# RWKV-6 attention with a gated MLP: a third unit's output projection by seven half-width products

## The chip, the cores and the metric

One Trainium2 chip, one core of it. The metric is device time in microseconds (us) of one execution of the whole program; lower is better. TensorE (PE) multiplies matrices, with PEld as its weight load; VectorE (DVE), ScalarE (ACT) and GpSimd (POOL) work on tiles; SyncE (SP) issues most of the transfers.

## The reference, cut to what matters

```python
# attention: batch 4, 8 heads, 768 tokens, head size 48
for t in range(S):
    kt, vt, rt, wt = (k[:, :, t], v[:, :, t], r[:, :, t], w[:, :, t])
    cur = np.einsum('bhd,bhe->bhde', u[None] * kt, vt)
    y[:, :, t] = np.einsum('bhd,bhde->bhe', rt, state + cur)
    state = wt[:, :, :, None] * state + np.einsum('bhd,bhe->bhde', kt, vt)
# bridge: x is y as 3072 tokens x 384
h = x @ w_in                                   # 384 -> 2048
sp = np.maximum(h, 0.0) + np.log1p(np.exp(-np.abs(h)))   # softplus
g = h * erf(sp)                                # the gate
return (g @ w_out).astype(np.float32)          # 2048 -> 384
```

All data is float32.

## The kernel before

**Units and steps.** The work is cut into 12 units of 256 tokens (128 tokens of two batches), taken in 12 steps, numbered from 0. Step s computes the attention of unit s. Beside it, the hidden layer of unit s - 1 is multiplied by w_in, its gate is computed, and the output projection (w_out) of unit s - 3 is done. So the third unit, number 2, is projected in step 5. Steps 0 to 4 go through the function attend, later ones through attend_late.

**The order is written out by hand.** Each engine takes its instructions in the order in which the program issues them. The attention of a step calls in_order (step 4) or run_late (later steps) at fixed places, and these work through short strings. In them "P" issues one piece of the projection, "H" one piece of the hidden layer (two of its 16 rows of blocks: 12 records of TensorE, then a copy on ScalarE, L1036), "s" and "e" a softplus and an erf of one chunk on ScalarE (L983, L987, each with a table load), "m" the multiplication of the gate on VectorE (L992), "F" the next part of the preparation of the following step, "S" the blends, "k" a copy of a quarter of the hidden layer into PSUM (L1100). "A" in step 4 advances a gate that is done in larger parts: softplus (L1009), erf (L1012), then the multiplication in two halves (L1016).

**Two ways to project.** Ordinarily (project) the 256 tokens x 2048 hidden values are multiplied by w_out in 32 matrix products, 384 columns wide, for each of the two batches into one PSUM tile; each tile is copied out on ScalarE (L1068) and sent. From unit FAST = 3 on, project_fast does it with seven products of half blocks instead of eight (Strassen's scheme in Winograd's form): 7 x 8 = 56 matrix products, 192 columns wide. For this

- the hidden values need four sums and differences of their quarters, the blends s1, s2, s3, s4 (L1119 to L1125, VectorE, 128x1024 each),
- the weights need three mixed tiles (L1083, on VectorE in step 3) and one difference in place, b12 - b11 in w_out_sb, which ends the use of the plain w_out_sb. It is sent by mixing.send to GpSimd in step 5, at the "G" of the last string,
- the results are partly added up outside PSUM. The two PSUM tiles m0 and m1 are read by copies on ScalarE (L1148, L1153, L1156) and by two additions on VectorE:

```python
        product(m0[:, lo], s3, t3, False)                                  # sixth product
        halves = o[1][:].rearrange("p (k n) -> p k n", k=2)
        nc.vector.tensor_add(halves, halves, m0[:, None, lo].to_broadcast([P, 2, ND]))   # L1162
        nc.sync.dma_start(out=out[i * NJ + 1, c], in_=o[1][:])
        yield
        if s < n_steps - 1:
            product(m1[:, lo], a12, b21, True)                             # seventh product
            nc.vector.tensor_add(o[0][:], o[0][:], m1[:])                  # L1167
```

The pool ps_m has two buffers ("m"). The projection holds both; after it, the first "H" piece of the step takes the buffer of m0 and the second that of m1, and so on in turn.

**Around the projection in a late step**, TensorE's order is: the level products (L557), the larger part of the projection, the last level's products (L557) and spread_blocks (L677), the rest of the projection, the state products (L664, which need kT from VectorE's L723), then eight "H" pieces (L1027, 96 records), and the attention's products with the values (L589). VectorE scales the inputs of the next step (L333), sums up its near terms (L458; GpSimd makes the terms with L468 and L472), and takes in by_tokens, a small table that goes through DRAM once the sums are complete (L506, L508, then L519). GpSimd also makes the totals (L407) and fades the state (L947, L964).

The functions that the change touches, as they are before:

Of the kernel before, what the change touches and what calls it, by code (L numbers as in the profile page):

```python
# [15 lines left out]
ALU = mybir.AluOpType  # L16

P = 128
FAST = 3
EP = 64  # L20
HC = 64
NC = 2
# [39 lines left out]
def kernel(  # L62
# [14 lines left out]
    nc = tc.nc  # L77
# [916 lines left out]
    def hidden(of, xT, gs, cut):  # L994


        def activate(h):

            held = []

            def softplus():
                n = 2 * (rooms["next"] % 2)
                rooms["next"] += 1
                held.append(
                    room[:, n : n + 2].rearrange("p i n -> p (i n)").rearrange(
                        "p (f t) -> p f t", t=UNIT
                    )
                )
                nc.scalar.activation(held[0], h[:], AF.Softplus)  # L1009

            def erf():
                nc.scalar.activation(held[0], held[0], AF.Erf)  # L1012

            def multiply():
                for part in (slice(0, FG // 2), slice(FG // 2, FG)):
                    nc.vector.tensor_mul(h[:, part], h[:, part], held[0][:, part])  # L1016

            later.extend([(softplus, True), (erf, True), (multiply, False)])

        for g in range(NG):  # L1020
            h = hid.tile([P, FG, UNIT], FP32, name="h")
            gs.append(h)
            for f in range(0, FG, FT):
                ps = ps_m.tile([P, FT, UNIT], FP32, name="m")
                for ff in range(FT):
                    for kk in range(KT):
                        nc.tensor.matmul(  # L1027
                            ps[:, ff, :],
                            lhsT=w_in_sb[:, g * FG + f + ff, kk * P : (kk + 1) * P],
                            rhs=xT[:, kk, :],  # L1030
                            start=kk == 0,
                            stop=kk == KT - 1,
                        )
                    if cut and not ff and g == NG - 1 and f == FG - FT:
                        yield
                nc.scalar.copy(h[:, f : f + FT, :], ps[:])  # L1036
                if of >= FAST:
                    if f % (2 * FT):
                        chunks.append(h[:, f - FT : f + FT])
                elif f == FG - FT:  # L1040
                    activate(h)
                yield
# [249 lines left out]
    def advance(count=None):  # L1292

        while later and count != 0:
            stage, last = later.pop(0)
            stage()
            count = count and count - 1
            if last and not count:
                break
# [20 lines left out]
    def in_order(s, k):  # L1320


        order = ("APPP", "APPP", "APPHH", "AHHH", "AHHH")
        for what in order[k]:
            if what == "A":
                advance()
            elif what == "P":
                piece(projs, s - 3)
            else:
                piece(hids, s - 1)  # L1330
# [2 lines left out]
    STAGES_LATE = ("front", "near", 0, 1, 2, 3, 4)  # L1333
    LATE = {
        DIRECT + 1: (
            "s ey", "m", "s ep m P P s ey m P P P", "s P F ep m P F P k22y k11p F", "S1",
            "S2 S3 H k12y S4 H F", "s H ep m H H F G s H H H ep",
        ),
        n_steps - 1: (
            "s P", "m w", "ey P m s P P ep P", "m P P", "", "", ""  # L1340
# [7 lines left out]
    def run_late(s, tokens, following=None):  # L1348

        for what in tokens.split():  # L1350
            if what == "A":
                advance()
            elif what == "P":
                piece(projs, s - 3)
            elif what == "H":
                piece(hids, s - 1)
            elif what == "F":
                next(following, None)
            elif what == "Q":
                piece(projs, s - 2)  # L1360
            elif what == "J":
                next(turns["joint"])
            elif what == "w":
                next(joining)
            elif what in "uvz":
                activate_pair(what)
            elif what == "T":
                join_tokens()
                turns["joint"] = hidden_of_two()
            elif what == "G":  # L1370
                mixing.send(nc.gpsimd)
            elif what == "s":
                softplus_chunk()
            elif what[0] == "e":
                erf_chunk(what[1])
            elif what == "m":
                multiply_chunk()
            elif what[0] == "k":
                to_lane(s - 2, what[1:3], what[3])
            else:  # L1380
                blend(s - 2, *(int(n) for n in what[1:]))
                if what == "S3":
                    del lanes["11"], lanes["22"]
                elif what == "S4":
                    del lanes["12"]
# [14 lines left out]
    mixing = mix_weights()  # L1400
# [9 lines left out]
    for kk in range(KT):  # L1410
        n = D // KT
        to, of = (x.rearrange("p (e m) -> p e m", e=NE) for x in (apart[:, kk], ident[:]))
        nc.vector.tensor_copy(out=to[:, :, D:], in_=of[:, :, kk * n : (kk + 1) * n])
    load_first()
    with tc.manual_schedule(
# [74 lines left out]
        s = n_steps  # L1490
# [108 lines left out]
```

## Time and profile before

| | us |
|---|---|
| median of three runs | 582.31 (582.29 to 584.92) |
| the profiled execution | 582.34 |
| its span in the trace | 580.6 |
| PE busy | 573.2 (99% of the span) |
| DVE busy | 443.9 (76%) |
| ACT busy | 354.9 (61%) |
| POOL busy | 277.9 (48%) |
| step 4 on TensorE, from its first level products to those of step 5 | 144.2 to 192.7 |
| step 5, from there to the end of its hidden layer | 192.7 to 237.9 |

The profile is of one execution. A line such as "L1027 PE MATMUL m<-xT,w_in_sb" names the line of the kernel, the engine, the operation and the tiles written and read. A float32 matrix product stands in the trace as two records, so 32 products are 64 records. In the chain that ended last, TensorE has 92%.

### The profile page before, as it was taken

The page shows a single profiled execution, that of the slowest core. Times are in us where ns is not written, and L with a number is a line of the kernel's source. Part 1 is how long each engine was busy: PE and PEld are TensorE (multiplying, and loading weights), DVE is VectorE, ACT ScalarE, POOL GpSimd, SP SyncE. Part 2 cuts the span into 40 slices and gives each one's busy share as a digit, 9 for nine tenths or more (in the row PEclk, how much of TensorE's full clock was granted, in tenths as well). Part 3 has the DMA queues.
Part 4 walks back from the last instruction along what each step waited for, and adds up shares of the span by engine and source line. Part 5 has one row for each costly group of instructions (what it writes and reads, how often), then busy time and mean ns, then how long its engine had stood idle before and what let it go on. Part 6 is the DMA issues. An engine that isn't in the chain of part 4 may idle for free.

```text
span 580.6 us, 16629 instructions
## 1 busy us (share of the span) xinstructions
PE 573.2 (99%) x7240; PEld 491.9 (85%) x7240; DVE 443.9 (76%) x539; ACT 354.9 (61%) x478; POOL 277.9 (48%) x313
## 2 busy tenths in 40 slices
PE   8999999999999999999999999999999999999997
PEld 6678887678578668998998898898898899988997
DVE  7775876999994899799799799699699637256640
ACT  3658777644444698766766766766666761388700
POOL 3557391703898389469369359459449100000000
PEclk9999999999999999999999999999999999999999
DMA  8596662340443414234334334333331301000000
GB/s 271 180 313 244 240 202 85 149 148 11 145 150 83 123 43 169 41 138 155 63 126 155 75 119 164 75 113 134 75 109 56 75 8 37 1 0 2 28 27 28
DMA packets 54081, 63.24 MB, mean 109 GB/s; under 512 B 35160, under 2 KB 40568, under 8 KB 52984
## 3 DMA queue, kind: packets, MB, share of 16 engines
q1 hardware_dynamic: 53624, 61.98, 33.4%
q8 instruction: 57, 0.93, 0.7%
q10 hardware_dynamic: 384, 0.20, 0.1%
q14 instruction: 16, 0.13, 0.1%
HBM read 52.39 MB, written 8.69 MB: 105 GB/s over the span
## 4 chain that ended last, share of the span: by engine, by line
PE 92%; DVE 4%; POOL 1%; DMA 1%; issue 1%; ACT 0%; SPq 0%; DVEq 0%; POOLq 0%; ACTq 0%
PE m L1027 34%; PE m L1142 28%; PE m L1059 9%; PE pp L557 5%; PE pp L1230 4%; PE y L1230 2%; PE y L589 2%; PE y L615 2%; PE pp L664 2%; PE m L864 1%; DMA words<-in_moe_w_in 1%; DVE in L333 1%; PE pp L873 1%; PE pp L940 1%; DVE rk L468 1%
## 5 line engine op out<-in xcount | busy, mean ns | idle before, releaser
L1027 PE MATMUL m<-xT,w_in_sb 128*128 128x256 f32 x960 | 215.2, 382 | 0.0
L1027 PEld LDWEIGHTS m<-xT,w_in_sb 128*128 128x128 f32 x960 | 179.9, 190 | 25.8 <-ACT h L1036 1.0
L333 DVE TENSOR_TENSOR in<-in,tot_sb 128x1024 f32<-128x1024 f32 (+1 forms) x55 | 75.2, 1367 | 14.1 <-PE pp L557 11.8
L468 POOL TENSOR_TENSOR rk<-words 128x528 f32<-128x528 f32 (+3 forms) x28 | 42.5, 1517 | 85.1 <-DVE sums L458 81.1
L1036 ACT COPY h<-m 128x512 f32<-128x512 f32 x80 | 46.3, 581 | 59.0 <-PE m L1027 58.9
L472 POOL TENSOR_TENSOR words<-words,rest 128x528 f32<-128x528 f32 (+10 forms) x77 | 78.1, 1014 | 6.0
L1059 PE MATMUL m<-w_out_sb,h 128*128 128x384 f32 x192 | 64.3, 491 | 0.0
L1059 PEld LDWEIGHTS m<-w_out_sb,h 128*128 128x128 f32 x192 | 35.8, 190 | 23.4
L1142 PE MATMUL m<-mixed,h 128*128 128x192 f32 x256 | 45.6, 332 | 0.0
L1142 PE MATMUL m<-w_out_sb,h 128*128 128x192 f32 x256 | 44.8, 329 | 0.0
L1142 PEld LDWEIGHTS m<-mixed,h 128*128 128x128 f32 x256 | 41.4, 190 | 0.9
L1142 PEld LDWEIGHTS m<-w_out_sb,h 128*128 128x128 f32 x256 | 41.6, 190 | 0.3
L1142 PE MATMUL m<-w_out_sb,room 128*128 128x192 f32 x240 | 41.5, 326 | 0.0
L557 PEld LDWEIGHTS pp<-in 48*48 48x48 f32 (+4 forms) x2368 | 30.1, 120 | 12.8 <-issue 5.6
L983 ACT ACT_TABLE_LOAD x30 | 38.5, 1283 | 2.8 <-issue 2.3
L1142 PEld LDWEIGHTS m<-w_out_sb,room 128*128 128x128 f32 x240 | 39.4, 190 | 0.0
L987 ACT ACT_TABLE_LOAD x30 | 38.5, 1283 | 0.5
L468 POOL TENSOR_TENSOR words<-words 128x336 f32<-128x336 f32 (+6 forms) x49 | 35.2, 718 | 3.8
L557 PE MATMUL pp<-in 48*48 48x32 f32 (+4 forms) x2368 | 33.9, 206 | 1.2 <-DVE in L333 1.1
L458 DVE TENSOR_REDUCE sums<-rk 128x14 f32<-128x672 f32 (+9 forms) x54 | 34.7, 701 | 0.0
L407 POOL TENSOR_TENSOR tot_sb<-tot_sb 128x256 f32<-128x256 f32 (+4 forms) x50 | 32.6, 652 | 3.8
L458 DVE TENSOR_REDUCE sums<-words 128x6 f32<-128x288 f32 (+8 forms) x66 | 27.4, 464 | 3.9 <-POOL words L468 3.6
(199 smaller groups left out, 949.8 us busy)
## 6 DMA issues: line engine op xcount, KB each, us to landing
in<-in_rkw SPq DMA_DIRECT2D x8, 1024.0 KB, 5.1
words<-in_moe_w_in SPq DMA_DIRECT2D x16, 384.0 KB, 5.2
words<-in_moe_w_out SPq DMA_DIRECT2D x16, 384.0 KB, 6.3
words<-in_rk_rows SPq DMA_DIRECT2D x8, 768.0 KB, 5.9
w<-in_rkw SPq DMA_DIRECT2D x11, 512.0 KB, 5.5
v<-in_v SPq DMA_DIRECT2D x12, 384.0 KB, 5.4
out<-o SPq DMA_DIRECT2D x23, 192.0 KB, 2.7
in<-in_rkw SPq DMA_DIRECT2D x7, 512.0 KB, 6.3
```

The costliest lines, as they stand in the source:

```text
L333: nc.vector.tensor_mul(halves, halves, view(tots[level - 1], 0, [[1, n], [2, nb], [0, half]]))
L458: nc.vector.tensor_reduce(out=view(sums[:], n, [[near * (NEAR + 1), NEAR // near], [NEAR + 1, near - n]]), in_=terms[n], axis=mybir.AxisLi ...
L468: engine.tensor_mul(terms[n], r[:, :, n:], k[:, :, : near - n])
L472: engine.tensor_mul(k[:, :, :m], k[:, :, :m], w[:, :, n : n + m])
L557: nc.tensor.matmul(to, lhsT=rk(1, n)[rows(e), s0 : s0 + m], rhs=right, start=True, stop=True,)
L983: nc.scalar.activation(sp_room, chunks[0], AF.Softplus)
L987: nc.scalar.activation(at, sp_room, AF.Erf)
L1027: nc.tensor.matmul(ps[:, ff, :], lhsT=w_in_sb[:, g * FG + f + ff, kk * P : (kk + 1) * P], rhs=xT[:, kk, :], start=kk == 0, stop=kk == KT - 1,)
L1036: nc.scalar.copy(h[:, f : f + FT, :], ps[:])
L1059: nc.tensor.matmul(ps[j][:], lhsT=gs[g][:, f, j * C : (j + 1) * C], rhs=w_out_sb[:, g * FG + f, :], start=g + f == 0, stop=g == NG - 1 and ...
L1142: nc.tensor.matmul(to, lhsT=a[:, f], rhs=b[:, f], start=start and f == 0, stop=f == FG - 1, skip_group_check=True,)
L1230: nc.tensor.matmul(to[:, e], lhsT=a[:, 2 * i + e], rhs=b, start=start and not k, stop=True, skip_group_check=True,)
```

## The change

The constant FAST becomes 2, so that unit 2, too, is projected by project_fast, in step 5. A second constant, CHUNKED = 3, keeps the gate of unit 2 as it was (in larger parts). The rest moves what project_fast needs:

- in step 4 the third place runs "APPAAHH" for "APPHH": the second erf is issued there, ahead of the two "H" pieces, and the last two gate multiplications follow at once; the fourth place issues the weight difference ("G", now to VectorE), the fifth the four blends ("B"), where the "A" for erf and multiplications stood;
- in step 5 the strings hold the seven pieces of the short projection for the eight of the ordinary one, and no "G" any more.

```diff
-FAST = 3
+FAST = 2
+CHUNKED = 3
...
-                if of >= FAST:
+                if of >= CHUNKED:
                     if f % (2 * FT):
                         chunks.append(h[:, f - FT : f + FT])
...
-        order = ("APPP", "APPP", "APPHH", "AHHH", "AHHH")
+        order = ("APPP", "APPP", "APPAAHH", "GHHH", "BHHH")
         for what in order[k]:
             if what == "A":
                 advance()
+            elif what == "G":
+                mixing.send(nc.vector)
+            elif what == "B":
+                blend(s - 2)
             elif what == "P":
                 piece(projs, s - 3)
...
         DIRECT + 1: (
-            "s ey", "m", "s ep m P P s ey m P P P", "s P F ep m P F P k22y k11p F", "S1",
-            "S2 S3 H k12y S4 H F", "s H ep m H H F G s H H H ep",
+            "s ey", "m", "P P P s ep m P s ey m P", "s P F ep m F P k22y k11p F", "S1",
+            "S2 S3 H k12y S4 H F", "s H ep m H H F s H H H ep",
         ),
...
-            elif what == "G":
-                mixing.send(nc.gpsimd)
```

Line numbers in the text are those of the kernel before. Instruction by instruction the two programs differ so: TensorE has the 56 half-width products in the place of 32 of full width; VectorE has the weight difference, four blends and two additions more, and two multiplications at another place; ScalarE has three copies (L1148, L1153, L1156) for two (L1068) and the one erf earlier; GpSimd loses the weight difference; SP's two output transfers come from L1163 and L1168.

## The prediction

> **What bounds the kernel now.** I read the page first, then the chain of waits in order of time, then the timelines of VectorE and ScalarE over steps 4 and 5. TensorE is busy for 99% of the span, so the change is worth what it takes from TensorE's row of work, less every hole that it tears into it. The page and then the chain (start, length, what):
>
> ```profile
> PE 573.2 (99%) x7240; PEld 491.9 (85%) x7240; DVE 443.9 (76%) x539; ACT 354.9 (61%) x478; POOL 277.9 (48%) x313
> ```
>
> ```profile
> 193.58 13.10 PE m L1059 x40
> ...
> 207.62 7.94 PE m L1059 x24
> 215.55 0.86 PE pp L664 x64
> 216.42 21.55 PE m L1027 x96
> ...
> 243.56 10.60 PE m L1142 x64
> ...
> 255.09 5.40 PE m L1142 x32
> ...
> 261.35 20.92 PE m L1027 x96
> ```
>
> The first four rows are step 5, the others step 6, which already has the short projection. The hidden layer took 21.55 in step 5, 20.92 in step 6: there are 0.6 us of holes in the former. VectorE's timeline, with the idle time before an instruction and what ended it in brackets:
>
> ```profile
> 170.77 3.85 DVE L1016 TENSOR_TENSOR h<-h,room 128x1024 f32<-128x1024 f32 x2
> ...
> 182.50 0.20 DVE L458 TENSOR_REDUCE sums<-words 128x1 f32<-128x48 f32 x1 [0.57 <-POOL words L468]
> ...
> 188.80 1.23 DVE L519 TENSOR_TENSOR own<-block_sb,by_tokens 128x1024 f32<-128x1024 f32 x1 [1.95 <-DMA by_tokens<-by_blocks]
> 189.94 2.50 DVE L1016 TENSOR_TENSOR h<-h,room 128x1024 f32<-128x1024 f32 x2
> 193.65 1.24 DVE L333 TENSOR_TENSOR in<-in,tot_sb 128x1024 f32<-128x1024 f32 x1 [1.22 <-PE pp L557]
> ...
> 213.52 2.13 DVE L333 TENSOR_TENSOR in<-in,w 128x1024 f32<-128x1024 f32 x1
> 216.98 1.22 DVE L992 TENSOR_TENSOR h<-h,pp 128x1024 f32<-128x1024 f32 x1 [1.33 <-ACT pp L987]
> 218.12 3.37 DVE L333 TENSOR_TENSOR in<-in,tot_sb 128x1024 f32<-128x1024 f32 x2
> ...
> 259.21 0.54 DVE L1162 TENSOR_TENSOR o<-o,m 128x384 f32<-128x384 f32 x1
> 259.68 1.72 DVE L333 TENSOR_TENSOR in<-in,w 128x1024 f32<-128x1024 f32 x1
> 261.32 0.54 DVE L1167 TENSOR_TENSOR o<-o,m 128x384 f32<-128x384 f32 x1
> ```
>
> What to see: between 193.65 and 216.98 VectorE never stops, so a delay at 193.65 is handed on in full; and in step 6 L1162 and L1167 lie 2.1 us apart, the second over before TensorE wants m1's buffer. ScalarE in step 5:
>
> ```profile
> 214.13 0.48 ACT L1068 COPY o<-m 128x384 f32<-128x384 f32 x1
> 214.62 1.28 ACT L987 ACT_TABLE_LOAD   x1
> 215.92 1.03 ACT L987 ACTIVATE pp<-room 128x1024 f32<-128x1024 f32 x1
> 216.88 0.47 ACT L1068 COPY o<-m 128x384 f32<-128x384 f32 x1
> ```
>
> The ordinary projection gives both PSUM buffers back by copies on ScalarE, at 214.6 and 217.4; the hidden layer wants the first at 216.35, the second 2.69 later, at 219.04. No hole.
>
> **The products.** Out go 13.10 + 7.94 = 21.04. In come five short ones in a row, 10.60 for four (step 6) and 2.60 for one more, 13.2, and two later, 5.40: 18.6. TensorE gains 2.44 and ends the state products at 213.9 instead of 216.35. On the way it needs s1 at 198.8 (below: written at 192.8) and, for the fourth product, m0 copied out by L1148: ScalarE is free at 201.10, copies for 0.30, TensorE comes at 201.41. At worst 0.1, and covered by the wait found below.
>
> **Step 4 on VectorE.** The second pair of gate multiplications moves from 189.94 to right behind the first pair, at 174.6. Its erf comes earlier too: 168.50 (after L1068) plus load 1.28 and 1.91 is 171.7, so no wait; the two hidden pieces behind it are copied up to 1.2 later, and TensorE wants those buffers from 174.62 on. Beside POOL's products a pair costs 3.85 (the first pair), while it cost 2.50 at its old place. VectorE itself has cover there: it waited 3.65 in all for POOL between 177.5 and 182.5. But POOL slows as well: its 128x288 products take 0.81 and 0.79 alone and 1.67 where VectorE multiplies beside them (220.49). Bounds for the delay of the last sum: 0 (POOL unhurt) and 1.9 (POOL loses half of 3.85). I take two products doubled, 0.86 + 0.8 = 1.6, as the first pair, the nearest row, did this to 128x336. The last sum then ends at 184.3, and by_tokens, 6.1 behind the sum (182.7 to 188.8), comes at 190.4.
>
> The weight difference, 1.76 on VectorE (the 128x1536 rows of step 3; on POOL it took 3.45), stands between the last sum and the state additions L961 and L965. With these, POOL's 0.83 between them and L333, VectorE is at by_tokens at about 189.4: hidden by the transfer, with 1 us to spare. Should it run beside POOL's L947 and stretch like the multiplications (1.22 to 1.93), it takes 2.8 and the cover is just used up.
>
> The blends follow L519: four at 1.14 to 1.26 (the moved pair's pitch), 4.9. VectorE ends them at 190.4 + 1.14 + 4.9 = 196.4 instead of being ready at 192.4 and starting L333 at 193.65. Delay D = 2.8; without POOL's 1.6 it is 1.2, with all stretched 3.4.
>
> [...]
>
> **Step 5, the new wait.** TensorE's first hidden piece now waits for L1162 and its second for L1167, both in VectorE's queue. L1162 stands behind L333 (212.92, 0.60): 213.52 + 2.8 = 216.3, done at 216.9. So the first piece starts at 216.9. TensorE could be there at 213.9, or at 214.4 since kT comes 2.8 later, at 213.5, and the state products (0.87) wait for it; either is covered by the wait for L1162. Behind L1162 there stand, in this step alone, three long instructions ahead of L1167: L333 from 216.8 for 2.05, the fourth chunk's L992 for 1.14, L333 for 1.63. L992 needs its erf: ScalarE's three new copies add 0.97 + 0.26 and the first L1068 (0.50) is gone, so 216.95 becomes 217.7; L992 starts at 218.8, not held by it. L1167 runs from 221.6 to 222.15. The second hidden piece starts at 222.2 where it started at 219.04; TensorE stands still for 2.6 (219.6 to 222.2). The seven pieces left take 2.69 + 5 x 2.59 + 2.69 = 18.3 and end at 240.5, against 237.90. The 0.6 of old holes do not come back, since ScalarE then leads TensorE.
>
> [...]
>
> **The rest.** GpSimd loses 3.45 after 229.5 and is later by D before: no one waits there. The output transfers leave SP at 216.9 and 222.2 instead of 214.6 to 217.7, and the loads behind them (rows and w) are 4.4 late; they are read only in step 6, from 241 on, 12 us after they land (222.2 and the 6.7 us that 768 KB took), or later. Behind step 5 all engines are later by about the same, and TensorE, without idle time, gets nothing back. Sum: 240.5 - 237.9 = 2.6 us. The profiled execution (582.34, 1.7 outside its span) becomes 584.9; the median of 582.31 says the same.
>
> **Rivals.** *The buffers come back in time, as in step 6*: then TensorE gains 2.44 and the 0.6 of old holes, 579.3. For it speaks that step 6 shows no hole with the same two additions; against it that L1167 would have to end by 216.6, while the erf ahead of it ends only at 217.7. Even with D = 0, L992 at 217.7 puts L1167's end at 217.7 + 1.14 + 1.63 + 0.54 = 221.0, a loss of 1.5. It takes a buffer that is not held after all. *VectorE's lag grows* (slower by more than the forecast): weight difference and blends stretch beside POOL's L947 and L407 as the multiplications do; from D = 3.1 on the loss passes 2.9, and with the pair at 1.9, the difference 1 late and blends at 1.5 D is 5, the loss 4.8: 587.1. For it: L407 took 2.54 at 185.21 and POOL and VectorE share that stretch; against: the old pair beside L407 took 1.25 each. *POOL is not slowed by the moved pair*: D = 1.2, L992 waits for the erf, loss 1.5: 583.8.
>
> **How the numbers follow.** A measurement tells about 0.5%, 2.9 us, from no change. Forecast with D between 1.2 and 3.1, a loss of 1.5 to 2.9, peak 2.6: 0.62, of which the unslowed POOL is 0.15. Growing lag: 0.32. Buffers in time: 0.06. So faster 0.06, within 0.5% 0.62, slower 0.32. The range from 582.9 to 586.4 leaves out the gain and the longest lag. The forecast is 584.9, a loss of 0.45%.
>
> **What would show it.** In the profile after: 80 and 32 records of L1142 in step 5 in some 13.2 and 5.4 us; a pair of L1016 near 174.6 with about 1.9 each and POOL's 128x288 products near 1.7; L519 near 190.4; L333 near 196.4; a hole of TensorE of about 2.5 us before the first hidden piece and of 2.6 before its second, ended by L1162 and L1167. I am wrong if the second hole is missing, if ScalarE ends it, or if a hole opens in the short products themselves (a blend late) or in step 6.

## The result, and the profile after

The changed kernel takes 586.2 us (median of seven runs, 584.84 to 588.55), the kernel before 582.29 in the same comparison (580.92 to 584.92). The ratio is 1.0066, with an interval of 1.004 to 1.0093: slower by 3.9 us. The profiled execution took 588.55, the longest of the seven; its span is 586.4. Line numbers after are one higher than before, up to some 1320.

Of the 5.8 us between the two spans, 1.45 lie ahead of step 5, which starts on TensorE at 194.145 instead of 192.699. They are put down to the run and not to the change: no edit acts before step 4, step 4 takes 48.7 us in both (it starts at 143.98 before and 145.43 after), and in the fourteen profiles of this case step 5 starts anywhere from 191.6 to 194.1. Where a time is said to be "moved back", 1.45 is taken off. The rest is step 5: from its first level products (L558) to its first products with the values (L590) it lasts 49.59 us, before 45.20. Every later step is as long as before (steps 6 to 10 take 44.3 in both, the rest of the run 121.2).

The page names the new wait in TensorE's costliest group; before, this group had no such wait:

```profile
L1028 PE MATMUL m<-xT,w_in_sb 128*128 128x256 f32 x960 | 216.9, 384 | 2.3 <-DVE o L1163 2.1
```

The chain that ended last (start, length, what) no longer runs along TensorE in step 5, as it did before. It goes through a transfer, and then through VectorE for 32 us:

```profile
186.42 2.27 DMA by_blocks<-sums
188.71 4.87 DMA by_tokens<-by_blocks
193.60 1.23 DVE own L520
...
215.33 1.63 DVE kT L724
...
224.89 0.47 DVE o L1168
225.41 18.40 PE m L1028 x84
```

VectorE's timeline (start, length, what, and in brackets the idle time before it and what ended it):

```profile
185.64 0.20 DVE L459 TENSOR_REDUCE sums<-words 128x1 f32<-128x48 f32 x1 [0.57 <-POOL words L469]
...
193.60 1.23 DVE L520 TENSOR_TENSOR own<-block_sb,by_tokens 128x1024 f32<-128x1024 f32 x1 [2.10 <-DMA by_tokens<-by_blocks]
...
199.68 1.23 DVE L334 TENSOR_TENSOR in<-in,tot_sb 128x1024 f32<-128x1024 f32 x1
...
219.75 0.54 DVE L1163 TENSOR_TENSOR o<-o,m 128x384 f32<-128x384 f32 x1
...
224.81 0.54 DVE L1168 TENSOR_TENSOR o<-o,m 128x384 f32<-128x384 f32 x1
```

What to see: the last sum ends at 185.85, and own starts 7.75 us later; before, it was 6.09. L334 starts at 199.68, moved back 198.23, instead of 193.65. Before, 1.22 of idle time stood ahead of it; now no bracket stands at it or behind it: VectorE is 4.6 us behind and never rests. L1163 and L1168 hold TensorE up, as the chain says for the second.

The windows of step 5 show what the chain does not (stretch, its length, then busy time and in brackets the instructions of TensorE, its weight load, VectorE, ScalarE and GpSimd, granted clock of TensorE, share and GB/s of the transfers):

```profile
214.10:217.60 3.50, 1.00 (x48) 0.73 (x50) 3.50 (x4) 2.67 (x3) 3.34 (x3) 0.99 0.03 7
217.60:221.00 3.40, 1.30 (x37) 1.05 (x27) 3.40 (x5) 2.31 (x2) 3.17 (x4) 0.50 0.38 114
221.00:224.40 3.40, 3.40 (x10) 2.68 (x9) 3.40 (x3) 1.36 (x2) 3.24 (x3) 0.50 0.19 64
```

TensorE's timeline has the holes of the step:

```profile
217.06 1.19 PE L665 MATMUL pp<-v,kT 64*48 64x48 f32 x64 [2.50 <-ACT room L984]
220.34 4.84 PE L1028 MATMUL m<-xT,w_in_sb 128*128 128x256 f32 x12 [2.10 <-DVE o L1163]
225.41 18.40 PE L1028 MATMUL m<-xT,w_in_sb 128*128 128x256 f32 x84 [0.23 <-DVE o L1168]
```

Two holes lie in the first two stretches, 2.5 us before the state products and 2.1 before the first hidden piece, which waits for L1163; 0.2 stand before the second piece. The profile puts the first hole down to ScalarE's L984, which ended at 216.80, but kT ended later, at 216.96: here, in e1, e4, e7 and e11 the state products start 0.10 after kT's end, so they are read as waiting for kT. From 217.6 to 224.4 the granted clock is 0.50, and the first hidden piece takes 4.84 us, 5.06 to the start of the second, instead of 2.69. Over step 5 TensorE was busy for 45.20 of 45.20 us before and for 44.77 of 49.59 after: 2.44 of work gone, 2.0 added by the slow clock, and 4.8 us of standing still.

### The profile page after: what moved, and what is told of

Same layout as the page of the kernel before. It is cut to its first block, busy times and chain, and to the rows that moved or that the text cites. A ratio compares the mean times of both kernels' runs of the same rounds, so it can differ in the third digit from the quotient of the medians.

```text
span 586.4 us, 16734 instructions
## 1 busy us (share of the span) xinstructions
PE 573.6 (98%) x7288; PEld 500.3 (85%) x7288; DVE 452.0 (77%) x546; ACT 355.6 (61%) x479; POOL 280.1 (48%) x312
## 4 chain that ended last, share of the span: by engine, by line
PE 61%; DVE 8%; issue 6%; POOL 6%; DMA 1%; ACTq 0%; ACT 0%; SPq 0%; POOLq 0%; DVEq 0%
PE m L1143 28%; PE m L1028 21%; PE pp L1231 4%; PE y L1231 2%; POOL words L473 2%; DVE in L334 1%; PE pp L558 1%; PE y L590 1%; DVE words L473 1%; PE y L616 1%; POOL words L469 1%; POOL rk L469 1%; DVE rk L469 1%; DVE sums L459 1%; PE pp L665 1%
## 5 line engine op out<-in xcount | busy, mean ns | idle before, releaser
L1028 PE MATMUL m<-xT,w_in_sb 128*128 128x256 f32 x960 | 216.9, 384 | 2.3 <-DVE o L1163 2.1
L334 DVE TENSOR_TENSOR in<-in,tot_sb 128x1024 f32<-128x1024 f32 (+1 forms) x55 | 75.7, 1377 | 12.5 <-PE pp L558 10.4
L1143 PE MATMUL m<-mixed,h 128*128 128x192 f32 x288 | 51.2, 331 | 0.0
L1143 PE MATMUL m<-w_out_sb,h 128*128 128x192 f32 x288 | 50.4, 329 | 0.0
L1143 PEld LDWEIGHTS m<-mixed,h 128*128 128x128 f32 x288 | 46.6, 190 | 1.0
L1143 PEld LDWEIGHTS m<-w_out_sb,h 128*128 128x128 f32 x288 | 46.8, 190 | 0.4
L1143 PE MATMUL m<-w_out_sb,room 128*128 128x192 f32 x272 | 47.0, 326 | 0.0
L1143 PEld LDWEIGHTS m<-w_out_sb,room 128*128 128x128 f32 x272 | 44.7, 190 | 0.0
L1060 PE MATMUL m<-w_out_sb,h 128*128 128x384 f32 x128 | 43.2, 492 | 0.0
L558 PEld LDWEIGHTS pp<-in 48*48 48x48 f32 (+4 forms) x2368 | 30.1, 120 | 11.8 <-issue 5.2
L1060 PEld LDWEIGHTS m<-w_out_sb,h 128*128 128x128 f32 x128 | 23.7, 190 | 15.4
L408 POOL TENSOR_TENSOR tot_sb<-tot_sb 128x256 f32<-128x256 f32 (+4 forms) x50 | 32.8, 656 | 3.8
L558 PE MATMUL pp<-in 48*48 48x32 f32 (+4 forms) x2368 | 33.9, 206 | 0.5 <-DVE in L334 0.4
L984 ACT ACTIVATE room<-h 128x1024 f32<-128x1024 f32 x28 | 29.6, 1057 | 0.3
```

The lines of the kernel that those rows point to most:

```text
L334: nc.vector.tensor_mul(halves, halves, view(tots[level - 1], 0, [[1, n], [2, nb], [0, half]]))
L558: nc.tensor.matmul(to, lhsT=rk(1, n)[rows(e), s0 : s0 + m], rhs=right, start=True, stop=True,)
L984: nc.scalar.activation(sp_room, chunks[0], AF.Softplus)
L1028: nc.tensor.matmul(ps[:, ff, :], lhsT=w_in_sb[:, g * FG + f + ff, kk * P : (kk + 1) * P], rhs=xT[:, kk, :], start=kk == 0, stop=kk == KT - 1,)
L1060: nc.tensor.matmul(ps[j][:], lhsT=gs[g][:, f, j * C : (j + 1) * C], rhs=w_out_sb[:, g * FG + f, :], start=g + f == 0, stop=g == NG - 1 and ...
L1143: nc.tensor.matmul(to, lhsT=a[:, f], rhs=b[:, f], start=start and f == 0, stop=f == FG - 1, skip_group_check=True,)
```

## The experiments

"Lag" is how far the first L334 behind own starts behind its 193.65, by a clock that puts the start of step 5 on TensorE at 192.70. "Step 5" and "step 6" are lengths on TensorE; these, the lag and the last column come from one profile of each kernel. The ratios are to the kernel before, measured beside it on the same chip, over all executions.

| kernel | ratio (interval) | step 5 | step 6 | lag | last sum to own |
|---|---|---|---|---|---|
| before | 1 | 45.20 | 44.30 | 0 | 6.09 |
| after | 1.0066 (1.004 to 1.0093) | 49.59 | 44.30 | 4.6 | 7.75 |
| e1_adds_together | 1.0073 (1.0052 to 1.0095) | 49.42 | 44.30 | 4.1 | 7.61 |
| e2_no_blends | 1.0059 (1.0038 to 1.008) | 48.48 | 44.30 | 0 | 7.59 |
| e3_no_blends_together | 1.0011 (0.9988 to 1.0033) | 46.12 | 44.30 | 0 | 7.69 |
| e4_blends_first | 1.0067 (1.0046 to 1.0088) | 48.88 | 44.30 | 3.3 | (blends between) |
| e5_filled | 1.0065 (1.0045 to 1.0084) | 48.55 | 44.30 | 4.1 | 7.61 |
| e6_pair_only | 1.0004 (0.999 to 1.0017) | 45.40 | 44.30 | 0 | 6.97 |
| e7_pair_back | 1.0075 (1.0053 to 1.0096) | 49.45 | 44.30 | 4.4 | 6.02 |
| e8_all_seven_first | 1.0048 (1.003 to 1.0067) | 48.08 | 44.30 | 4.8 | (blends between) |
| e9_kT_first | 1.0038 (1.0024 to 1.0052) | 46.74 | 45.00 | 3.3 | (blends between) |
| e10_filled_less | 1.0063 (1.0048 to 1.0078) | 48.62 | 44.30 | 4.2 | 7.68 |
| e11_fetch_earlier | 1.0161 (1.012 to 1.0203) | 48.94 | 44.30 | 3.8 | 7.11 |
| e12_seventh_behind | 1.0045 (1.003 to 1.006) | 46.43 | 44.88 | 3.3 | (blends between) |

### Which wait of step 5 costs

**e1_adds_together**: the sixth and seventh product in one go, so that L1168 stands right behind L1163 in VectorE's queue.

```diff
-"s P F ep m F P k22y k11p F"
+"s P P F ep m F k22y k11p F"
```

> Of step 5 only the string of the last level changes: the sixth and seventh piece of the projection follow each other, so that on VectorE L1167 stands right behind L1162, ahead of L333, the fourth chunk's L992 and L333. TensorE's order is the same. Theory A (the second hidden piece waits for L1167, whose place costs): that wait goes; the first piece still starts at the end of L1162, 26.2 us after step 5 begins on TensorE. At full rate the third piece is then held about 0.5 by ScalarE, and the kernel takes 1.9 less than the changed one, about 584.3. Theory B (it is the slow clock after the hole: in the changed kernel ten records of the first hidden piece came 0.427 apart for 0.216, which the wait for L1167 hid): the first piece stays slow, the second starts 4.6 behind it instead of 2.7, and only 0.4 is won, 585.8. Theory C (the lag D alone sets the loss): no gain, 586.2.

L1163 and L1168 now ran at 217.55 and 218.01, and the wait for L1168 was gone. Next to nothing was gained (0.17 in the step, and nothing in the time), since the clock took its place. TensorE's timeline:

```profile
214.86 0.94 PE L665 MATMUL pp<-v,kT 64*48 64x48 f32 x64 [2.05 <-issue]
218.15 10.15 PE L1028 MATMUL m<-xT,w_in_sb 128*128 128x256 f32 x33 [2.35 <-DVE o L1163]
```

The first twelve of those records took 5.28 us, at a granted clock of 0.50 from 216.9 to 223.8. So in the changed kernel the slow clock costs nothing of its own: L1168 would hold TensorE up until the same moment. Take that wait away, and the clock has it. (And take the clock away as well, and ScalarE has most of it: e5, below.)

**e2_no_blends**: unit 2's blends are left out, so that its output is wrong, and the weight difference goes back to GpSimd in step 5.

```diff
-        order = ("APPP", "APPP", "APPAAHH", "GHHH", "BHHH")
+        order = ("APPP", "APPP", "APPAAHH", "HHH", "BHHH")
...
-                blend(s - 2)
+                blend(s - 2, 0)
...
-            "S2 S3 H k12y S4 H F", "s H ep m H H F s H H H ep",
+            "S2 S3 H k12y S4 H F", "s H ep m H H F G s H H H ep",
```

> Leaves out the four blends of unit 2 and puts the weight difference back to GpSimd in step 5, so unit 2's output is not the reference's; TensorE, ScalarE and the order in step 5 are those of the changed kernel. VectorE's lag D then is 0 to 0.3. Theory C (D alone): TensorE has its gain, 2.4 to 3.0 below the kernel before, about 579.5. Theory A: L1162 is in time (no hole of over 0.3 before the first piece), but L1167 stands behind the fourth chunk's L992, whose erf ends about 25.1 after the step's start on TensorE: the second piece starts at 28.4 at the earliest, a hole of about 4, and the kernel is 1.5 above the one before, about 583.8.

With no lag there was no hole over 0.2 before the first piece, and one of 4.2 us before the second, since L1168 still stands behind the fourth erf and its multiplication. TensorE's timeline:

```profile
222.16 20.08 PE L1028 MATMUL m<-xT,w_in_sb 128*128 128x256 f32 x84 [4.17 <-DVE o L1168]
```

That is a loss of 3.28 in the step without any lag, 1.7 of it again half clock. Theory A had this wait right (the second piece 28.4 after the step's start, measured 28.47) and lacked the clock alone.

**e3_no_blends_together**: both edits.

> The two edits together (no blends of unit 2, which leaves its output wrong, and L1167 right behind L1162). Neither lag nor L1167's place is left. If that was all, the kernel is 2.4 to 3.0 below the one before, 579.3 to 579.9. If ScalarE's queue is next (its copies of the hidden pieces, L1036, stand behind the fourth erf and two L1100, and end at 28.8 after the step's start, while the third piece wants its buffer at 26.6), a hole of about 2 opens before the third piece and the gain is 0 to 0.8: 581.5 to 582.3.

Step 5 lasted 46.12: no hole over 0.2 before the first two pieces, 2.0 before the third and 0.7 before the fourth. ScalarE's timeline there:

```profile
218.74 1.02 ACT L1101 COPY y<-h 128x1024 f32<-128x1024 f32 x1 [1.29 <-DVE h L993]
219.69 1.01 ACT L1101 COPY pp<-h 128x1024 f32<-128x1024 f32 x1
220.73 0.59 ACT L1037 COPY h<-m 128x512 f32<-128x512 f32 x1
```

And TensorE's, which waits for the last of these copies:

```profile
221.37 2.86 PE L1028 MATMUL m<-xT,w_in_sb 128*128 128x256 f32 x12 [2.02 <-ACT h L1037]
```

The first piece was ready for its copy at 216.6. In ScalarE's queue it stood behind the erf and two copies for the blends of unit 3. Before, TensorE came 2.44 later, and the same order cost it next to nothing. Without lag and without the late L1168 the gain of the short projection was thus used up by the next queue.

### Where the lag comes from

**e4_blends_first**: the blends run while VectorE waits for by_tokens, ahead of own.

```diff
-"GHHH", "BHHH"
+"GHHH", "HHH"
...
+        if s == DIRECT:                 # in attend, behind the state additions
+            next(following, None)
+            blend(s - 2)
...
+        if s == DIRECT + 1:             # where the sums are followed by own: stop here once
+            yield
```

> The changed kernel, with the four blends ahead of L519 (which waits for by_tokens) instead of behind it; the rest is the same. Theory A with D: VectorE blends in the 2.1 us in which it waited, by_tokens is in time for it, D falls from 4.6 to about 2.4, and so do both holes: 2.1 less than the changed kernel, about 584.1. If the wait for by_tokens was not on the way: 586.2.

The lag fell to 3.3, not to the 2.4 that the filled idle time promised: beside GpSimd's L408 the blends took 1.22, 1.95, 1.52 and 1.42, 6.1 in all, instead of 4.9. Of the 1.3 less lag, 0.9 was left where VectorE reached L1163 and 0.7 at the end of the step. The first piece ran at half clock again and took 5.27, but this cost little of its own: L1168 came only 0.3 before its end. The time shows no gain at all.

**e6_pair_only**: the kernel before with only the gate pair moved.

```diff
-        order = ("APPP", "APPP", "APPHH", "AHHH", "AHHH")
+        order = ("APPP", "APPP", "APPAAHH", "HHH", "HHH")
```

> The kernel before, with only the last gate pair moved into the third stretch of the fourth step; the third unit's projection stays the ordinary one, with no weight difference and no blends. Theory: beside the pair GpSimd's term products slow down, the last sum ends 1.6 us later than 182.71 (by a clock of the run that starts step 5 at 192.70), and by_tokens, begun that much later, runs into the 16 KB packet of instructions that is fetched at about 189.9, so that it takes 4.8 us from its issue instead of 3.2; L519 then starts at 192.0 and ends at 193.3, still just ahead of the 193.65 at which the next multiplication follows TensorE: the lag stays under 0.3 us and the time at 582.3 +- 0.7. Rival (the landing is late for a reason of the new projection or of its weights, not for when it starts): by_tokens takes 3.2 us, L519 starts at 190.4; the time is the same, so the row decides, not the time.

By the common clock the last sum ended at 184.42, 1.7 later than before, so the pair does slow GpSimd. by_tokens took 4.1 from its issue to own, not 3.2 and not 4.8; the last of its 64-byte packets came 3.65 after the issue (before: 2.49). VectorE had cover, and nothing changed in time.

**e7_pair_back**: the change, with the pair back at the end of step 4.

```diff
-        order = ("APPP", "APPP", "APPAAHH", "GHHH", "BHHH")
+        order = ("APPP", "APPP", "APPHH", "AGHHH", "ABHHH")
```

> The changed kernel with the last gate pair back in the fifth stretch of the fourth step, right ahead of the blends; weight difference, blends and projection as in the change. Theory: the last sum ends at 182.7 (by a clock that starts step 5 at 192.70), by_tokens is out of the way of the instruction fetch and takes 3.2 us from its issue, GpSimd's fading product L948 is still slowed to 2.3 us by the weight difference beside it; own at 188.8 to 190.0, the pair 2.5, the blends 4.9: the next multiplication starts at 197.4, a lag of 3.7 instead of 4.58. Both holes in step 5 are then 0.9 shorter, the clock still falls to half behind them: step 5 lasts 48.7 (after: 49.59), the run 585.6. Rival (by_tokens lands late whenever it starts): it takes 4.8, own comes at 190.4, the lag is 5.4, step 5 lasts 50.4, the run 587.3.

```profile
187.79 1.62 DVE L520 TENSOR_TENSOR own<-block_sb,by_tokens 128x1024 f32<-128x1024 f32 x1 [0.36 <-DMA by_tokens<-by_blocks]
```

by_tokens was issued at 184.63 and took 3.16: it does not land late by itself. But the lag stayed at 4.4, since beside L408 own now took 1.62 and the pair 2.97 (before 1.23 and 2.50, beside L407), and the blends came behind them. The move of the pair thus cost nothing on balance, and bringing it back earns nothing; VectorE has the same work to do either way.

**e11_fetch_earlier**: eight tiny products at the very start of TensorE's program.

```diff
         stay_warm(6)
+        ps = ps_m.tile([P, NC, P], FP32, name="m")
+        for _ in range(8):
+            nc.tensor.matmul(ps[:, 0, :1], lhsT=ident[:], rhs=ident[:, :1], start=True, stop=True)
```

> The changed kernel with eight more products of one column on TensorE right at its start (identity times one column of identity; nobody reads them). They cost under 1 us there and move every later instruction of TensorE eight places down its program, so that its blocks of instructions (16 KB each, one packet on the instruction queue) are fetched earlier against the work: in the changed kernel one is fetched 1.95 us after by_tokens is issued, amid its packets; eight products are some 32 instructions, 3 to 3.5 us of the hidden pieces that run then. Theory 'fetch in the way': that fetch now comes before by_tokens is issued, by_tokens takes 3.2 us from its issue instead of 4.89, own starts 6.1 us after the last sum instead of 7.75, the lag is 2.9 to 3.1 us instead of 4.58, step 5 lasts 47.9 to 48.5 us instead of 49.59, the run some 584.9 us. Rival (by_tokens is slow for another reason, such as where its tensors lie or what GpSimd and VectorE do beside it): own still starts 7.6 to 7.8 us after the last sum, step 5 lasts 49.4 to 49.7, the run as in the change, 586.2.

What the fetch is, first in the view of the DMA queues, over the time from the issue of by_tokens to own. Its columns are packets, MB and the share of 16 engines' time. Before (185.6 to 188.8) there is one queue:

```profile
q1 hardware_dynamic: 3134, 0.34, 76.7%
```

After (188.7 to 193.6) there are two:

```profile
q1 hardware_dynamic: 4052, 0.51, 71.3%
q8 instruction: 1, 0.02, 1.2%
```

One packet of 16 KB on the instruction queue, of which there are 57 in the run. Before it came 4.3 us after by_tokens was issued, after the change 1.95, because by_tokens had moved 1.7 later and the packet came 0.7 earlier by the common clock. In e11 it came 3.3 us ahead of by_tokens, which then took 3.13 from its issue at 189.19, as VectorE's timeline says:

```profile
192.32 1.23 DVE L520 TENSOR_TENSOR own<-block_sb,by_tokens 128x1024 f32<-128x1024 f32 x1 [1.45 <-DMA by_tokens<-by_blocks]
```

Instead the packet met by_blocks, which took 3.41 to the issue of by_tokens, where it is 2.28 to 2.29 in every other kernel here. So the delay moved with the packet: by_tokens 1.76 shorter, by_blocks 1.12 longer. The lag fell to 3.8 and step 5 by 0.65, about half of what was expected. Eight products more at the start of TensorE's program thus moved the packet from 1.95 behind the issue to 3.3 ahead of it. Over all fourteen kernels the last 64-byte packet of by_tokens came 2.4 to 2.5 us after its issue where no instruction packet fell on it (before, e7, e11), and 3.6 to 3.8 after where one fell 1.5 to 2.4 us behind the issue (the eleven others). The time of this kernel, though, 590.12 (586.77 to 594.89), is far above its profiled step, and its runs show mean clocks from 0.977 to 0.997: the longer the run, mostly, the lower. Why the mean clock fell in these runs was not followed up and stays open.

### The clock

**e5_filled** and **e10_filled_less**: e1 with six, then three, idle products in the hole before the state products.

```diff
         ps = products([P, NC, JP, HC], 0)
+        if s == DIRECT + 1:
+            for _ in range(6):          # e10: 3
+                nc.tensor.matmul(       # ps: the first 384 columns
+                    ..., lhsT=ident[:], rhs=ident[:, None, :].to_broadcast([P, 3, P]), ...)
```

> The kernel of e1_adds_together with six more products of 128x384 on TensorE (identity times identity, into the bank that the state products then overwrite), put where TensorE waits 2.4 us for kT ahead of the state products. They add work that nobody needs and take no wait away: kT still comes when it comes, and the first hidden piece still waits for the add L1163. Theory 'clock' (two stretches of idle close together bring the granted clock to half for some 5 us): the clock stays at 1.00 from 215 to 224 us, the twelve products of the first hidden piece take 2.7 instead of 5.28 us, step 5 on TensorE lasts 46.6 to 47.4 us instead of 49.42, the run some 584.2 us. Theory 'only the waits count' (the half clock has another reason, such as the kind of product that comes next): the first piece still takes 5.3, step 5 lasts 49.4, the run 586.4.

> e5_filled with three filling products instead of six: there the six took 3.9 us and held the state products up by 2.0 us, so that the run showed the clock and the first hidden piece at full speed, but not the time. Three take 1.95 us, less than the 2.2 us of idle time ahead of the state products. Theory 'clock': granted clock 1.00 from 213 to 224 us, first hidden piece 2.7 us, the wait for L1163 of some 2.2 us still there, step 5 lasts 46.6 to 47.2 us (e1_adds_together: 49.42; e5_filled: 48.55), the run 583.6 to 584.4. Theory 'only the waits count': step 5 lasts 49.4, the run 586.4.

TensorE's timeline, the fill of e5:

```profile
213.79 4.14 PE L740 MATMUL pp<-ident 128*128 128x384 f32 x12
```

And the first pieces of e10, behind their wait:

```profile
218.58 5.62 PE L1037 MATMUL m<-xT,w_in_sb 128*128 128x256 f32 x17 [2.31 <-DVE o L1172]
```

In e5 the fill was too long by 2.0 us and left only 0.4 of a hole before the first piece. The clock stayed at 1.00 and the first piece took 2.69: with the fill, and TensorE busy for 5.61 of the 6.00 us from 215 to 221, no half clock came. Yet step 5 lasted 48.55, 0.87 less than in e1, for 2.6 saved in that piece. The fill did not take the rest (e10's expectation has it so, wrongly): the first piece started 25.73 us after the start of the step, in e1 25.75, at the end of L1163 in both. The next queue took it, at the fourth piece and in small holes behind. TensorE's timeline in e5:

```profile
228.34 13.73 PE L1037 MATMUL m<-xT,w_in_sb 128*128 128x256 f32 x60 [0.97 <-ACT h L1046]
```

In e10 the hole of 2.31 stayed, and my expectation failed: the clock fell to 0.50 all the same, for one spell of 3.4 us, from 219.95 on, and the first piece took 3.98. A second hole is not needed. In e3 a hole of 2.0 had left the clock alone. The two holes lay differently. In the clock table of the changed kernel's trace the spells of half clock are 3.413 us long (from 26.411) and 6.827 (from 217.557), and the full clock between them lasts 187.733, 55 times 3.413. In steps of this length, the hole of e10 lay, all but 0.3 us, inside one stretch (216.5 to 219.9, TensorE busy for 0.40 of it); that of e3 lay across the border of two (at 219.8; busy for 2.94 of 3.40 us ahead of it and for 1.93 of 3.50 behind). Whether this is what set the two apart is not shown by any run. The two windows of e10, with the columns as above:

```profile
216.54:219.95 3.41, 1.37 (x6) 1.24 (x7) 3.41 (x5) 2.18 (x2) 3.25 (x3) 1.00 0.54 172
219.95:223.36 3.41, 3.41 (x9) 2.70 (x9) 3.31 (x4) 2.04 (x3) 3.25 (x3) 0.50 0.95 293
```

### Ways around the lag

**e8_all_seven_first**: blends first, by e4's edits; the weight difference to GpSimd in step 4; in step 5 all seven products ahead of the last level, hidden copies ahead of the blends' copies.

```diff
-        order = ("APPP", "APPP", "APPAAHH", "GHHH", "BHHH")
+        order = ("APPP", "APPP", "APPAAHH", "HHH", "HHH")
...
+        if s == DIRECT:                 # in attend, behind GpSimd's second fading product
+            mixing.send(nc.gpsimd)
...
-            "s ey", "m", "P P P s ep m P s ey m P", "s P F ep m F P k22y k11p F", "S1",
-            "S2 S3 H k12y S4 H F", "s H ep m H H F s H H H ep",
+            "s ey", "m", "P P P s ep m P s ey P P P m s", "F ep m F F", "H k22y k11p S1",
+            "S2 S3 H H k12y S4 F", "s H ep m H F s H H H ep",
```

> The changed kernel with three orders altered and no work left out. (1) In step 4 the blends run ahead of own (as in e4_blends_first), and the weight difference goes to GpSimd behind its second fading product. (2) In step 5 all seven half-width products run ahead of the last level's products, so that the adds L1163 and L1168 stand right behind the second gate multiplication, some 2 us ahead of the hidden pieces that wait for them. (3) ScalarE copies the first hidden piece ahead of its two copies for the blends of the fourth unit, and the third ahead of the last such copy. Theory (the lag on VectorE and then ScalarE's queue are what ate the gain of the shorter projection): lag 1.8 to 2.1 us instead of 4.58, no hole over 0.5 us ahead of the state products or of any hidden piece, clock 1.00, step 5 lasts 43.0 to 43.8 us (before: 45.20), and with up to 0.8 us of it given back in step 6, where the sums on GpSimd come 2 us late, the run lasts 580.2 to 581.4 us, faster than both. Rival (another queue comes next, as in e3_no_blends_together, where 2.4 us of the gain went to ScalarE): a new hole of 1 to 3 us in step 5 or 6, and a time of 582 to 584.

The lag was 4.8. VectorE's timeline shows where:

```profile
187.18 3.97 DVE L334 TENSOR_TENSOR in<-in,tot_sb 128x1024 f32<-128x1024 f32 x1
```

And GpSimd's, beside it:

```profile
186.63 3.44 POOL L1091 TENSOR_TENSOR w_out_sb<-w_out_sb 128x1536 f32<-128x1536 f32 x1
```

L334 takes 1.22 in the kernel before; here it ended 1.08 after GpSimd's instruction did. The weight difference on GpSimd cost VectorE 2.75, more than the 1.82 that it takes VectorE itself. The step was 48.08.

**e9_kT_first**: e4's step 4; kT and L1163 ahead of the sums in VectorE's queue.

```diff
-        next(following, None)           # in attend_late, ahead of the product of kT
+        if s != DIRECT + 1:
+            next(following, None)
...
+            "s ey", "m", "P P P s P ep P s ey P F P m m s", "F ep m F F", "H H k22y k11p S1",
+            "S2 S3 H k12y S4 F", "s H ep m H F s H H H ep",
```

> The changed kernel with step 4 as in e4_blends_first (the blends ahead of own, the weight difference on VectorE as in the change) and step 5 in another order, no work left out: all seven half-width products ahead of the last level's products; on VectorE the multiplication of kT and the add L1163 ahead of the sums of the near terms, the add L1168 right behind them; on ScalarE the first two hidden copies ahead of its copies for the fourth unit's blends. Theory (VectorE's lag and then ScalarE's queue ate the gain; both can be stepped around): the lag is 3.3 us as in e4_blends_first, yet kT, L1163 and L1168 end before TensorE asks for them (some 3.4 us ahead of it, at the time it asks, and 1 us ahead of it); no hole over 0.5 us, clock 1.00, step 5 lasts 43.0 to 43.8 us (before: 45.20); step 6 gives back 0 to 1 us, since the sums on VectorE and own come some 1.3 us later in it; the run 580.3 to 581.6 us. Rival (the gain is lost again in a queue not seen yet, or in full in step 6): step 5 over 44.5 us, or step 6 longer by over 1.5 us, and a time of 582 to 584.

kT was ready at 210.0, 4 us early, and both additions came before TensorE asked for their buffers. A hole of 2.3 opened before the state products all the same, since they take the PSUM bank that ScalarE had not yet emptied. TensorE's timeline, then ScalarE's:

```profile
216.31 1.53 PE L667 MATMUL pp<-v,kT 64*48 64x48 f32 x64 [2.28 <-ACT own L577]
```

```profile
212.73 1.28 ACT L990 ACT_TABLE_LOAD   x1
...
215.10 1.16 ACT L577 COPY own<-pp 32x512 f32<-32x512 f32 x2
```

I had put the softplus ahead of these copies. Half clock behind the hole took 0.9 more in the first piece. The step was 46.74, and step 6 0.70 longer than before.

**e12_seventh_behind**: e9 without this wait; the last level ahead of the seventh product, the softplus behind the copies.

```diff
-            "s ey", "m", "P P P s P ep P s ey P F P m m s", "F ep m F F", "H H k22y k11p S1",
+            "s ey", "m", "P P P s P ep P s ey P F", "P m m s F", "H ep m F F H k22y k11p S1",
```

> e9_kT_first with the hole of its step 5 mended, no work left out: what held its state products up was not kT but ScalarE, whose two copies of the last level stood behind a softplus. Here the last level's products run ahead of the seventh half-width product, which covers those copies; the fourth softplus stands behind them, and the first hidden copy ahead of the fourth erf. Theory 'VectorE has no room left' (in e9_kT_first own of step 6 came at 241.7 to 242.9, whatever TensorE did in step 5): no hole over 0.7 us in step 5, which lasts 42.6 to 43.3 us (before: 45.20), but own of step 6 still ends 49 us or more after the start of step 5 on TensorE, a lag of some 4 to 5 us there, and step 6 (first own product of step 6 to that of step 7) lasts 47 to 48.5 us instead of 44.30: the run 583 to 585. Rival (VectorE catches up, since TensorE waits for it nowhere else): step 6 lasts under 45.2 us, and the run 580.0 to 581.2 us, faster than before.

The first five hidden pieces ran without a hole from 214.84 on, 21.2 us after the start of step 5 (before: 23.65). The gain was there, and 3.3 us were lost at the sixth piece; without that hole the step would have been 43 us long. TensorE's timeline:

```profile
231.57 8.56 PE L1034 MATMUL m<-xT,w_in_sb 128*128 128x256 f32 x36 [3.30 <-ACT h L1043]
```

ScalarE's, whose copies stand behind this one:

```profile
227.66 1.02 ACT L1107 COPY y<-h 128x1024 f32<-128x1024 f32 x1 [2.38 <-DVE room L1126]
```

And VectorE's in step 6:

```profile
241.40 1.23 DVE L522 TENSOR_TENSOR own<-block_sb,by_tokens 128x1024 f32<-128x1024 f32 x1 [3.00 <-DMA by_tokens<-by_blocks]
```

ScalarE stood still for 2.4 us, because its copy for unit 3's blends overwrites the PSUM room that VectorE's first blend (L1126) reads, and that blend came late. own of step 6 ended 49.0 us after the start of step 5, as the first theory said. It starts 47.8 after it here, 48.0 and 48.2 in e8 and e9, 46.6 to 47.5 in the seven other kernels with the blends, 43.7 in e2 and e3 without them and 42.8 in the kernel before: the order of step 5 hardly moves it, the work added to VectorE in step 4 does (e2 and e3 leave out both the blends and the weight difference, and the share of each was not told apart). The theory was right on VectorE and wrong on the place: two thirds of the loss (1.23 of 1.81) came in step 5 already. No version with all the work done was faster than before.

## Why the prediction was right, and which term was not

The forecast was 2.6 us slower, the measurement 3.9. At 586.2 it lies just inside the range, which ends at 586.4, and by the prediction's own division it belongs to its rival of the growing lag (a loss from 2.9 us on, chance 0.32) rather than to the forecast. The mechanism was right: VectorE's lag, handed on to the two additions that give the buffers back. That the range held was in part luck: the prediction's sum turns the measured lag of 4.6 into a loss of 4.4, which is what step 5 shows in the profile (49.59 for 45.20) and would be 586.7; the median came 0.5 lower. Point by point, by the common clock:

- **Products**: 13.2 and 5.4 came as said, the fourth product was not held up.
- **The pair in step 4**: 1.92 and 1.82 an instruction beside GpSimd's products, not the 1.21 of L992 before at 203.09, where GpSimd was idle; these, 128x288, took 1.67 and 1.66, and the last sum ended at 184.40 (said: 184.3). e7, without the move, has it at 182.66.
- **Weight difference**: 1.82, hidden. It pushed GpSimd's L948 from 0.83 to 2.35 and the state additions with it; e7, where by_tokens was on time, shows that only 0.36 of the cover was left.
- **by_tokens, 6.1 behind the sum**: this is the term that was mis-sized. It was 7.75. The transfer was carried over as a constant, but 1.7 later it ran into a packet of instructions. 1.65 of the 1.8 that the lag was larger (4.6 for 2.8) is this term. Of it, 1.2 is the last 64-byte packet (3.70 after the issue for 2.49); own started another 0.45 further behind that packet than before, and no run shows why.
- **Blends**: 4.94 (said: 4.9), and not stretched, so the rival of the growing lag had the right size and the wrong cause.
- **Step 5**: the first piece at 218.9 (said: 216.9), the second at 224.0 (said: 222.2), the end at 242.3 (said: 240.5): all three late by 1.8 to 2.0, the excess of the lag and little more. The order of the waits, kT under L1163 and then L1168, was as said, and the seven pieces behind took 18.3.
- **The sign of being wrong**: a missing second hole was to show it, and the second hole is 0.23 us for 2.6. The wait for L1168 was there all the same; the half clock stretched the first piece over it, from 2.69 to 4.84.
- **A misreading**: VectorE does stop between 193.65 and 216.98, for 1.33 ahead of the latter, as that row says. The sum did not use it: it lets the late L333 cover this idle time, as it did.
- **Rivals**: that the buffers come back in time was ruled out rightly; e2, without any lag, still loses 3.3.
- **Not foreseen**: the half clock behind the holes. The wait for L1168 covered it, so that leaving it out did no harm here: luck, not foresight. In e1, where that wait is gone, the first piece took 5.28 for 2.69.

The 2.44 that the shorter products save never reached the end of the step, which took 49.59 for 45.20. But e12 shows that the two buffers were only the first of the queues, and VectorE the last that was found.

## What to carry to other kernels

Before shortening the busiest engine's work, ask what each engine that feeds it will have to do in the time that is left: here 2.4 us of TensorE were bought with 6.8 us on VectorE (blends and weight difference), which had no room for it once TensorE came earlier, and every reordering tried here only moved the wait from one queue to the next. Don't carry a transfer's latency over as a constant when its start moves (here by_tokens took 3.22 us from its issue to own before, 4.89 after): look at what else the DMA queues carry at the new time. And count a hole of two microseconds in TensorE as up to four (an estimate: e10's 2.3, and 1.7, half of the 3.41 us at half clock behind it), until the granted clock of the windows behind it has been read.

## What the runs showed of the hardware

- **Half clock came behind stretches with idle time of TensorE.** A hole of 2.3 us (e10) brought a spell of 3.41 us at half clock, one of 2.0 (e3) brought none. In stretches of some 3.4 us, those with TensorE busy for 0.94 of 3.40 us (e1, from 213.5), 1.00 of 3.50 and 1.30 of 3.40 (after, from 214.1 and 217.6) and 1.37 of 3.41 (e10, from 216.54) were followed by half clock, and so was one with 2.14 of 3.40 (after, from 23.0); one with 1.93 of 3.50 (e3, from 219.8) was not, and neither was one with 2.49 of 3.40 (after, from 19.6). No one border of busy time fits all of these. The same kernel ran at a mean clock of 1.000 in some executions and below it in others: the runs of e3 with a mean clock of 1.000 took 581.8 to 583.9, those with 0.996 to 0.999 took 581.9 to 583.8, those with 0.994 took 585.7 and 586.0. What decides it there is not shown, as only one of these runs was profiled.
- **The start of the profiled execution after** has such a spell too: from 26.4 to 29.8 us the clock was 0.50, behind a stretch in which TensorE was busy for 2.14 of 3.40. It can have cost at most 1.7 us, half its length; how much of the 1.45 by which step 5 starts later it makes up is not shown, as other kernels' profiles start that step up to 1.1 us earlier or later than before without such a spell.
- **An instruction fetch got in the way of the kernel's own small transfers**: one packet of 16 KB, 0.98 us long after the change, went with a delay of 0.9 (e6) to 1.7 us (after) for a table of 128 KB, and in e11 the delay moved with the packet.
- **Beside a long instruction of the other engine, VectorE and GpSimd were stretched** in two rows by nearly the whole time that the two lay side by side: L948 by 1.52 us of 1.65, e8's L334 by 2.75 of 2.89. VectorE's weight difference and GpSimd's L948 in the changed kernel:

```profile
185.76 1.82 DVE L1084 TENSOR_TENSOR w_out_sb<-w_out_sb 128x1536 f32<-128x1536 f32 x1
185.93 2.35 POOL L948 TENSOR_TENSOR faded<-s,tot_sb 128x384 f32<-128x384 f32 x1
```

  L948 (0.83 before, as L947) ended 0.69 after the weight difference, and e8's L334 (1.22 before) 1.08 after GpSimd's. The price is not always that: the blends beside L408 kept 1.22 to 1.31 after the change and took up to 1.95 in e4.
